# Float16 parts for the first 64 queries of later pairs, bfloat16 products for the scales, and averaged planning deadlines

## The chip, the cores and the metric

The kernel runs on one core of a Trainium2 chip. The metric is the device time of one execution in microseconds. A core has five engines that run side by side: PE (TensorE, matrix products), DVE (VectorE), ACT (ScalarE), POOL (GpSimd) and SP (SyncE, which issues the DMA transfers here). Each engine works through its own instructions in the order in which they were written.

## The reference

Eight batches of eight heads do causal attention over 576 positions of 64 values, with a bias that falls with the running sum of `s`. The result goes through two dense layers with an ELU between them.

```
scores = q @ k.T / 8 + min(-(cum[i] - cum[j]), 0)      # causal, cum = cumsum(max(s, 0))
attn   = softmax(scores)
x      = (attn @ v) with the heads side by side          # 4608 rows of 512
h      = x @ w_in                                        # 512 -> 2048
g      = where(h > 0, h, exp(min(h, 0)) - 1)
out    = g @ w_out                                       # 2048 -> 512, float32
```

## The kernel before

**Arithmetic.** PE takes a float32 product in a slower form than a float16 one. Nearly all products are therefore made from float16 parts: a number is multiplied by a power of two, its rounded float16 value is the high part, what is left over is the low part, and three products (high by high, high by low, low by high) are summed in PSUM. The power of two comes from the largest absolute value of the data.

**Scales.** `scales_of` (L713 on) finds such a power. DVE reduces columns of peaks into one column of `tops` (L723), PE multiplies `tops` by the identity matrix so that the 128 partitions' maxima lie in one row (`flat`, L734), DVE takes the maximum and builds the power of two from its exponent bits (`own`, L726 to L730), PE multiplies a matrix of ones by it so that every partition has it (`every`, L737), and DVE copies it to a column of `scales` (L739). Both products are float32, and the trace shows a float32 product as two matmul records. There are 13 calls: 3 for the early batches, 1 for the weights, 9 for groups of values.

**Attention.** Heads are worked in pairs. For the first three batches (`Low`) the first 320 queries run in float32. For the other five (batches 3 to 7) the first 64 queries of both heads make a unit of their own (`u.h is None`): 20 units. Such a unit scores one 128 by 128 block (`sc_None`, L1141), takes the softmax (`psh_None`, normalised at L1162 to L1166 by whichever engine the planner picks), transposes it on PE (`tr_None`, L1294), splits the transposed block into a rounded part and a rest in the type float32r (`split_pt`, `pc_None`, L1227), and multiplies both by the values (`av_None`, L1287). The values `vs_None` are a rounded part and a rest too (`rounded` at L488 to L490, `rest` at L508 and L509). `halves` (L1350 on) then adds the part that was multiplied by the rounded values to the part multiplied by the rest: a copy (L515) and an addition (L1356) for each head. The later queries run with float16 parts: their probabilities go through DMA transposes (L481) and come back as `T`, which meets the values `v` in `av` (L1328).

**Dense layers.** The 4608 rows are cut into 18 chunks of 256. The first chunk runs in float32 while the weights are still being converted, the others with three float16 products (`h` at L1503, `o` at L1560). The activation between them takes ACT (L1515, L1539) and DVE (L1535, L1542).

**The order of the work.** All of this is first written down as operations (`Plan.op`), each with the engines that could do it and a cost for each. `Plan.run` is a list scheduler: it takes the operation that could start first, and among those of the same engine that could start by then the one with the earliest latest-start time `late`. `Plan.deadlines` works those times out backwards from the end of a finished run. `Plan.issue` does this in rounds:

```
for n in range(self.ROUNDS):                     # 8
    end, order = self.run(False)
    if best is None or end < best[0]:
        best = end, self.wait, [(o, o.late) for o in self.ops]
    self.deadlines(order, end)
```

The times under which the planned end was earliest are used once more to write the instructions out. So every instruction's place in the queue of its engine depends on the costs of all operations. In the first 60 us PE also runs products that nobody reads (`scratch`, L1623), placed where the plan leaves it idle.

Of the kernel before, what the change touches and what calls it, by code (L numbers as in the profile page):

```python
# [93 lines left out]
class Op:  # L94
    __slots__ = ("ways", "after", "before", "behind", "bufs", "new", "prio", "ready", "left", "filler", "late", "at", "frees")


class Plan:
# [45 lines left out]
    def op(self, prio, ways, reads=(), writes=(), late=()):  # L144
# [44 lines left out]
        o.left, o.ready, o.late = len(o.after) + len(firsts), {}, 0.0  # L189
# [21 lines left out]
    def deadlines(self, order, end):  # L211

        late = dict.fromkeys(self.ENDS, end)
        for o in reversed(order):
            engine, start, stop, lag = o.at
            t = late.get(engine, end)
            for d in o.before:
                if d.at is not None:
                    t = min(t, d.late - lag - self.HOPS.get((engine, d.at[0]), self.HOP))
            for b in o.bufs:  # L220
                for d in b.followed:
                    t = min(t, d.late - lag - self.HOPS.get((engine, d.at[0]), self.HOP))
            t -= stop - start
            for d in o.behind:
                if d.at is not None:
                    t = min(t, d.late)
            o.late = t
            if engine in late:
                late[engine] = t

    ENDS = ("PE",)
    ROUNDS, WAIT = 8, {"PE": 0.0, "DVE": 0.0, "ACT": 0.0, "Pool": 0.0, "SP": 0.0}

    def issue(self):
        best = None
        for n in range(self.ROUNDS):
# [7 lines left out]
        for o, late in lates:  # L244
            o.late = late
# [3 lines left out]
    def run(self, emit):  # L249
# [24 lines left out]
        while pending:  # L274
# [13 lines left out]
            for o in pending:  # L288
# [31 lines left out]
                key=lambda x: (x[4].late, x[1]))  # L320
# [76 lines left out]
def act_s(n):  # L397

    return 205 + n / 1.2
# [17 lines left out]
def pool_1(n):  # L417

    return 255 + 0.87 * n
# [8 lines left out]
def kernel(  # L428
# [55 lines left out]
    def rounded(prio, n, dst, src, reads, writes, sign=1.0, only=None):  # L484

        ways = [
            ("Pool", pool_1(n),
             lambda: pool.tensor_scalar(dst(), src(), sign, 1.0, ALU.mult, ALU.mult)),  # L488
            ("ACT", act_s(n),
             lambda: act.activation(dst(), src(), AF.Copy, scale=sign)),  # L490
            ("DVE-SB", dve_1(n),
             lambda: dve.tensor_scalar(dst(), src(), sign, None, ALU.mult)),
        ]
        op(prio, [w for w in ways if only is None or w[0] in only], reads, writes)

# [8 lines left out]

    def rest(prio, n, dst, src, hi, reads, writes, only=None):

        ways = [
            ("DVE-SB", dve_2(n), lambda: dve.tensor_tensor(dst(), src(), hi(), ALU.subtract)),  # L508
            ("Pool", pool_2(n), lambda: pool.tensor_tensor(dst(), src(), hi(), ALU.subtract)),  # L509
        ]  # L510
        op(prio, [w for w in ways if only is None or w[0] in only], reads, writes)
# [163 lines left out]
    all_ones = plan.buf(const, [P, P], F32, "all_ones")  # L675
# [7 lines left out]
    def scale_tiles():  # L683
# [4 lines left out]
        op(-8, [("Pool-M", 150.0, lambda: pool.memset(all_ones.v, 1.0))], [], [all_ones])  # L688

# [23 lines left out]
    def scales_of(prio, spans, dst):  # L713
# [6 lines left out]

        def largest():
# [3 lines left out]
        def exponents():  # L725
# [4 lines left out]
            dve.tensor_scalar(own.v[:, :n], ident[:, :n], own.v[:, 3:4], None, ALU.mult)  # L730
# [366 lines left out]
    def prepare(u):  # L1097
# [17 lines left out]
        src, used = (lambda: u.va.v[:, j, :1]), values_of(u.va, j)  # L1115
        rounded(prio, D, lambda: u.vs.v[:, :1, 0], src, used, [u.vs])
        rest(prio, D, lambda: u.vs.v[:, :1, 1], src,
             lambda: u.vs.v[:, :1, 0].bitcast(F32), used, [u.vs])
# [105 lines left out]
    def split_pt(prio, tag, tr, w):  # L1224
        pc = plan.buf(sb, [P, 2, w], F32R, f"pc_{tag}", tag="pc")
        psum_copy(prio, w, lambda: pc.v[:, 0], lambda: tr.v[:, :w], [tr], [(pc, 0)])
        op(prio, [("DVE", dve_p(w), lambda: dve.tensor_tensor(  # L1227
            pc.v[:, 1], tr.v[:, :w], pc.v[:, 0].bitcast(F32), ALU.subtract))],
# [3 lines left out]
    def scoring(u):  # L1232
# [8 lines left out]
        if u.h is None:  # L1241
# [3 lines left out]
            def pair():  # L1245
# [6 lines left out]
                    (sm, 0, True, 1, 1.0), view=lambda v: v.rearrange("p (h t) -> p h t", h=2),  # L1252
# [26 lines left out]
    def weighing(u):  # L1279
# [11 lines left out]
        if u.h is None:  # L1291
            def pair():
# [4 lines left out]
                products(pe(P), [  # L1297
                    ([pc, u.vs], lambda pc=pc, m=m: (
                        u.vs.v.rearrange("p n a d -> p n (a d)")[:, 0], pc[0].v[:, m]))
                    for m, pc in enumerate(pieces)], slice(P), True, True)  # L1300
                for h in range(2):
                    halves(prio, h, HB, u.x_part((h, 0)), 0, av, h * HB)
# [47 lines left out]
    def halves(prio, h, n, dst, c0, av, a0):  # L1350
# [3 lines left out]
        cols, here = slice(c0, c0 + n), slice(a0, a0 + n)  # L1354
# [375 lines left out]
```

## Time and profile before

| what | value |
|---|---|
| median of 3 runs | 1020.91 us (1017.25 to 1024.87) |
| the profiled execution | 1021.47 us |
| its span, first to last instruction | 1019.7 us |
| PE busy | 997.2 us, 98% of the span |
| DVE busy | 846.5 us, 83% |
| ACT busy | 660.1 us, 65% |
| POOL busy | 261.1 us, 26% |
| mean granted TensorE clock | 0.998 of full speed |

PE is the engine that is nearly always busy. A matmul's record lasts longer than the time until the next matmul can start, because matmuls are pipelined; what a product costs is therefore read from the distance between starts, not from the mean duration. A busy share of 98% leaves about 22 us in which the profile sees PE do nothing, and the stretches in which they lie matter more than their sum.

### The profile page before, as it was taken

The numbers are of one execution on the slowest core, as the hardware profiler recorded it, in microseconds if no ns is written. First come the engines' busy times: TensorE is split into PE (matmuls) and PEld (weight loads), VectorE is DVE, ScalarE is ACT, GpSimd is POOL, SyncE is SP. The second block draws the span as 40 slices with busy tenths as digits, with TensorE's granted clock in tenths as the row PEclk, the third lists the DMA queues.
The fourth block names the chain that finished last, engine by engine and source line by source line (L and its number), as shares of the span: only waits on it lengthen the run. The fifth ranks groups of instructions, "written<-read, shape, count | busy, mean of one in ns | idle before, by whom it ended". The sixth has DMA issues, their size and how long they took to land.

```text
span 1019.7 us, 21777 instructions
## 1 busy us (share of the span) xinstructions
PE 997.2 (98%) x7327; PEld 686.5 (67%) x7327; DVE 846.5 (83%) x2352; ACT 660.1 (65%) x1583; POOL 261.1 (26%) x429
## 2 busy tenths in 40 slices
PE   8999999999989999999999999999999999999998
PEld 7677666666656666666666666666766666666665
DVE  6899899989989898999998998898979898744343
ACT  5999776776667676676776777666657665533232
POOL 6332272423232323322222222221412330100000
PEclk9999999999999999999999999999999999999999
DMA  7888743688999997899889999989979998521000
GB/s 205 251 256 274 208 130 87 133 224 162 195 205 205 225 224 178 191 223 214 184 181 225 199 185 203 239 185 240 189 177 217 204 210 180 92 69 43 1 22 21
DMA packets 296724, 179.83 MB, mean 176 GB/s; under 512 B 209908, under 2 KB 270564, under 8 KB 296612
## 3 DMA queue, kind: packets, MB, share of 16 engines
q1 hardware_dynamic: 296612, 178.45, 76.6%
q8 instruction: 57, 0.93, 0.4%
q14 instruction: 55, 0.45, 0.1%
HBM read 93.08 MB, written 36.81 MB: 127 GB/s over the span
## 4 chain that ended last, share of the span: by engine, by line
PE 45%; DVE 4%; DMA 2%; issue 1%; ACT 1%; SPq 0%; DVEq 0%; ACTq 0%
PE h L1503 19%; PE o L1560 19%; PE sc L1141 3%; PE av L1328 3%; DMA T<-p 1%; DVE p L1209 1%; DVE p L1144 1%; DMA stq<-in_qT_dram 0%; DVE gg L1542 0%; DVE h L1535 0%; DMA spread<-parts 0%; ACT p L1149 0%; DVE p L1203 0%; DVE parts L1064 0%; ACT g L1522 0%
## 5 line engine op out<-in xcount | busy, mean ns | idle before, releaser
L1503 PE MATMUL h<-xh,wp 128*128 128x256 f16 x2176 | 401.5, 273 | 0.0
L1560 PE MATMUL o<-wp,gg 128*128 128x512 f16 x1632 | 391.2, 379 | 4.1 <-DVE tops L723 1.5
L1503 PEld LDWEIGHTS <-wp 128*128 128x128 f16 x3264 | 317.4, 98 | 66.1 <-issue 1.3
L1503 PE MATMUL h<-xl,wp 128*128 128x256 f16 x1088 | 296.9, 273 | 0.0
L1560 PEld LDWEIGHTS <-gg 128*128 128x128 f16 x1632 | 156.8, 98 | 152.8 <-DVE gg L1542 5.9
L1149 ACT ACTIVATE p<-p,mn 128x192 f32<-128x192 f32 (+1 forms) x232 | 144.0, 621 | 80.1 <-DVE mn L1144 77.5
L1209 DVE SCALAR_TENSOR_TENSOR p<-p,sm,p 128x512 f16<-128x512 f32 (+3 forms) x258 | 155.1, 630 | 3.4 <-ACT p L1205 1.5
L1515 ACT ACTIVATE g<-h,cs 128x512 f32<-128x512 f32 x136 | 92.4, 679 | 77.1 <-PE h L1503 75.5
L1539 ACT ACTIVATE gg<-h 128x512 f16<-128x512 f32 x127 | 75.4, 593 | 85.5 <-DVE h L1535 84.7
L1542 DVE SCALAR_TENSOR_TENSOR gg<-h,gg 128x512 f16<-128x512 f32 x136 | 93.2, 685 | 25.0 <-ACT gg L1539 24.5
L1141 PE MATMUL sc<-set 128*128 128x288 f16 (+3 forms) x544 | 109.7, 298 | 2.9 <-DVE mn L1144 1.6
L1144 DVE CUSTOM_DVE_ANT_0 p<-sc,maskw 128x192 f32<-128x192 f32 (+1 forms) x232 | 108.6, 480 | 4.2 <-PE sc L1141 1.8
L1535 DVE SCALAR_TENSOR_TENSOR h<-g,cs,h 128x512 f32<-128x512 f32 x136 | 101.9, 749 | 9.1 <-ACT g L1522 5.2
L1201 POOL TENSOR_SCALAR p<-p,sm 128x512 f16<-128x512 f32 (+3 forms) x78 | 53.6, 691 | 217.6 <-DVE sm L1155 80.3
L1205 ACT ACTIVATE p<-p,sm 128x512 f16<-128x512 f32 (+3 forms) x152 | 79.1, 532 | 26.5 <-ACT p L1149 8.3
L1526 DVE TENSOR_SCALAR g<-g 128x512 f32<-128x512 f32 x81 | 36.3, 448 | 58.1 <-ACT g L1515 57.7
L1141 PEld LDWEIGHTS <-set 128*128 128x128 f16 x584 | 55.1, 98 | 35.8 <-issue 6.0
L1328 PEld LDWEIGHTS <-v 128*64 128x64 f16 x960 | 48.5, 111 | 24.4 <-issue 13.7
L1328 PE MATMUL av<-T,v 128*64 128x256 f16 (+5 forms) x960 | 62.3, 281 | 2.1 <-DMA T<-p 2.0
L500 POOL TENSOR_SCALAR v<-va,scales 128x320 f16<-128x320 f32 (+1 forms) x41 | 25.3, 620 | 98.7 <-PE av L1328 66.8
L500 POOL TENSOR_SCALAR xh<-xc,cs 128x512 f16<-128x512 f32 x22 | 16.7, 760 | 130.0 <-PE h L1503 127.0
L1149 ACT ACTIVATION_READ_ACCUMULATOR p<-p,mn 128x1 f32 x232 | 43.6, 188 | 0.0
(205 smaller groups left out, 1271.2 us busy)
## 6 DMA issues: line engine op xcount, KB each, us to landing
set<-spread SPq DMA_DIRECT2D x32, 432.0 KB
spread<-parts_None SPq DMA_DIRECT2D x32, 288.0 KB
set<-spread SPq DMA_DIRECT2D x32, 288.0 KB
raws<-in_w_in_dram SPq DMA_DIRECT2D x16, 512.0 KB
raws<-in_w_out_dram SPq DMA_DIRECT2D x16, 512.0 KB
out_dram<-ost SPq DMA_DIRECT2D x32, 256.0 KB
va<-in_vb_dram SPq DMA_DIRECT2D x16, 352.0 KB
xc<-x_dram SPq DMA_DIRECT2D x22, 256.0 KB
```

The costliest lines, as they stand in the source:

```text
L1141: pe_.matmul(view(sc.v[:, :cw]), l, r, start=n == 0, stop=n == len(pairs) - 1)
L1144: op(prio, [("DVE", 168 + cw + 55 * (i > 0), lambda i=i, sc=sc: dve.tensor_tensor_reduce(pt.v[:, i * cw : (i + 1) * cw], sc.v[:, :cw], mv( ...
L1149: op(prio, [("ACT", 383 + w / 1.2, lambda: act.activation(pt.v[:, :w], pt.v[:, :w], AF.Exp, bias=mn.v[:, n - 1 : n], scale=-1.0, accum_out ...
L1205: ("ACT", 295 + size / 1.2, lambda part=part: act.activation(part(0), own(part), AF.Copy, scale=sm.v[:, r])),
L1209: ("DVE-SB", dve_2(size), lambda part=part: dve.scalar_tensor_tensor(part(1), own(part), sm.v[:, r], part(0), ALU.mult, ALU.subtract)),
L1328: pe_.matmul(av.v[w.h * HB : (w.h + 1) * HB, dst], w.values.v[:, w.h, kb, v], part(w, kb, m), start=kb == 0 and m == 0 and v == 0, stop=kb ...
L1503: pe_.matmul(columns(k), weight_part(f, 0, part)[1]()[:, c * P : (c + 1) * P], xx.v[:, c], start=(c == 0 and m == 0), stop=(c == NCB - 1 a ...
L1515: op(side, [("ACT", act_c(W) + (0 if native else 90), lambda: act.activation(g.v, hp.v, AF.Exp, scale=1.0 if native else by(3)))], [hp] + ...
L1535: op(side, [("DVE", dve_p(W) + 60, lambda: dve.scalar_tensor_tensor(hp.v, g.v, by(2 if sign[0] else 1), hp.v, ALU.mult, ALU.max))], [g, cs ...
L1539: ("ACT", act_c(W), lambda: act.activation(gg.v[:, 0], hp.v, AF.Copy, scale=2.0**-DOWN)),
L1542: op(side, [("DVE", dve_p(W), lambda: dve.scalar_tensor_tensor(gg.v[:, 1], hp.v, 2.0**-DOWN, gg.v[:, 0], ALU.mult, ALU.subtract))], [hp, ( ...
L1560: pe_.matmul(acc[i].v, gg.v[:, g, at], weight_part(f, 1, part)[1](), start=(f == 0 and m == 0), stop=(f == NF - 1 and m == 2),)
```

## The change

Three things are edited.

1. `scales_of` takes only the upper 16 bits of each maximum (a bfloat16 with the same exponent) and multiplies by a bfloat16 identity `ident16`, a new tile that POOL fills once. The power of two is kept in bfloat16 too, and `all_ones` becomes bfloat16. Each of the two products becomes one matmul of 16-bit data.
2. The 20 first-64 units go to float16. The probabilities carry a factor `UP` of 2^15, the values the group's scale `u.col`, so `vs` now waits for that column of `scales`. Their low part is made by DVE alone (it was DVE or POOL). `pc` is float16 and has its own buffer tag `pt16` in place of the one that it shared with `psh`. `halves` multiplies by the inverse scale in both of its steps.
3. The planner sorts by `due`, which is the mean of the earlier `due` and the new `late` from the second round on, runs 10 rounds in place of 8, and leaves the unread products out of the deadlines.

```
 def deadlines(self, order, end):
...
-                if d.at is not None:
+                if d.at is not None and not d.filler:
...
-    ROUNDS, WAIT = 8, {"PE": 0.0, "DVE": 0.0, "ACT": 0.0, "Pool": 0.0, "SP": 0.0}
+    ROUNDS, WAIT = 10, {"PE": 0.0, "DVE": 0.0, "ACT": 0.0, "Pool": 0.0, "SP": 0.0}
...
-                best = end, self.wait, [(o, o.late) for o in self.ops]
+                best = end, self.wait, [(o, o.due) for o in self.ops]
             self.deadlines(order, end)
+            for o in order:
+                o.due = o.late if not n else (o.due + o.late) / 2
...
-                key=lambda x: (x[4].late, x[1]))
+                key=lambda x: (x[4].due, x[1]))
...
-    all_ones = plan.buf(const, [P, P], F32, "all_ones")
+    all_ones = plan.buf(const, [P, P], BF16, "all_ones")
+    ident16 = plan.buf(const, [P, P], BF16, "ident16")
...
+        def powers():
+            return own.v.bitcast(BF16)[:, :n]
...
-            dve.tensor_scalar(own.v[:, :n], ident[:, :n], own.v[:, 3:4], None, ALU.mult)
+            dve.tensor_scalar(powers(), ident[:, :n], own.v[:, 3:4], None, ALU.mult)
...
-        op(prio, [("PE", pe4(P), lambda: pe_.matmul(flat.v[:, :P], tops.v, ident, start=True, stop=True))],
-           [tops], [flat])
+        op(prio, [("PE", pe16(P) + 60.0, lambda: pe_.matmul(
+            flat.v[:, :P], tops.v.bitcast(BF16)[:, 1::2], ident16.v, start=True, stop=True))],
+           [tops, ident16], [flat])
...
-        op(prio, [("PE", pe4(P), lambda: pe_.matmul(every.v[:, :n], all_ones.v, own.v[:, :n], start=True, stop=True))],
+        op(prio, [("PE", 90.0, lambda: pe_.matmul(every.v[:, :n], all_ones.v, powers(), start=True, stop=True))],
...
-        u.vs = plan.buf(sb, [P, 1, 2, D], F32R, f"vs_{u.tag}", tag="vs0", bufs=NP)
+        u.vs = plan.buf(sb, [P, 2, D], F16, f"vs_{u.tag}", tag="vs0", bufs=NP)
...
+        by = lambda: scales.v[:, u.col : u.col + 1]
+        scaled(prio, D, lambda: u.vs.v[:, 0], src, by, used, [(u.vs, 0)])
+        op(prio, [("DVE-SB", dve_2(D), lambda: dve.scalar_tensor_tensor(
+            u.vs.v[:, 1], src(), by(), u.vs.v[:, 0], ALU.mult, ALU.subtract))], [*used, (u.vs, 0)], [(u.vs, 1)])
...
-        pc = plan.buf(sb, [P, 2, w], F32R, f"pc_{tag}", tag="pc")
+        pc = plan.buf(sb, [P, 2, w], F16, f"pc_{tag}", tag="pt16")
...
-                products(pe(P), [
-                    ([pc, u.vs], lambda pc=pc, m=m: (
-                        u.vs.v.rearrange("p n a d -> p n (a d)")[:, 0], pc[0].v[:, m]))
+                products(pe16(P) + 30.0, [
+                    ([pc, (u.vs, 0), (u.vs, 1)], lambda pc=pc, m=m: (
+                        u.vs.v.rearrange("p a d -> p (a d)"), pc[0].v[:, m]))
...
-        psum_copy(prio, n, lambda: x.v[own, cols], lambda: av.v[other, here], [av], [dst])
-        op(prio, [("DVE", dve_p(n), lambda: dve.tensor_tensor(
-            x.v[own, cols], av.v[own, here], x.v[own, cols], ALU.add))], [av], [dst])
+        op(prio, [
+            ("ACT", act_c(n) + 90, lambda: act.activation(
+                x.v[own, cols], av.v[other, here], AF.Copy, scale=scales.v[other, back])),
+            ("DVE", dve_p(n), lambda: dve.tensor_scalar(
+                x.v[own, cols], av.v[other, here], scales.v[other, back], None, ALU.mult)),
+        ], [av, (scales, back.start)], [dst])
+        op(prio, [("DVE", dve_p(n) + 60, lambda: dve.scalar_tensor_tensor(
+            x.v[own, cols], av.v[own, here], scales.v[own, back], x.v[own, cols], ALU.mult, ALU.add))],
+           [av, (scales, back.start)], [dst])
```

## Rows read from the trace of the kernel before

**Rows 1.** The page, busy us (share of the span) and instructions of PE

```profile
PE 997.2 (98%) x7327; PEld 686.5 (67%) x7327; DVE 846.5 (83%) x2352; ACT 660.1 (65%) x1583; POOL 261.1 (26%) x429
```

**Rows 2.** Stretches: busy PE, PEld, DVE, ACT, POOL (instructions), granted clock, DMA share, GB/s

```profile
0.00:75.00 75.00, 69.52 (x482) 55.14 (x483) 62.69 (x212) 58.82 (x184) 34.37 (x90) 1.00 0.82 237
150.00:200.00 50.00, 47.79 (x361) 33.14 (x361) 48.84 (x141) 34.71 (x93) 19.55 (x28) 1.00 0.49 110
200.00:300.00 100.00, 95.44 (x706) 63.44 (x705) 90.11 (x271) 67.78 (x170) 32.84 (x47) 1.00 0.92 197
300.00:800.00 500.00, 495.79 (x3812) 338.79 (x3810) 451.00 (x1277) 346.75 (x822) 127.22 (x191) 1.00 0.94 204
800.00:900.00 100.00, 97.98 (x773) 68.13 (x772) 80.72 (x208) 58.68 (x121) 18.48 (x29) 0.98 0.80 168
```

**Rows 3.** Waits of PE: us in total, times, longest us

```profile
PE sc L1141 <- DVE mn L1144: 3.0, 5, 0.8
PE tr_None L1294 <- ACT psh_None L1166: 2.2, 1, 2.2
PE av L1328 <- DMA T<-p: 2.0, 1, 2.0
```

**Rows 4.** Lines of PE, the unread products: busy us, mean ns | idle before

```profile
L1623 PE MATMUL scratch<-ident 128*128 128x128 f32 x138 | 20.1, 301 | 0.0
```

**Rows 5.** Products of the first 64 queries: duration ns min/median/max, first and last start

```profile
L1287 PE MATMUL av_None<-pc_None,vs_None x40: 272/292/412, 161.6 to 609.8; 128*128 128x128 f32 x40
```

**Rows 6.** Timeline of PE around 363 us: start us, us, what

```profile
363.22 0.27 PE L1503 MATMUL h<-xl,wp 128*128 128x256 f16 x1
363.33 0.27 PE L1503 MATMUL h<-xh,wp 128*128 128x256 f16 x1
363.36 0.42 PE L1287 MATMUL av_None<-pc_None,vs_None 128*128 128x128 f32 x2
363.61 0.29 PE L1503 MATMUL h<-xh,wp 128*128 128x256 f16 x1
```

**Rows 7.** Timeline of PE and its weight loads at 286.4 us

```profile
286.40 0.28 PE L1141 MATMUL sc_None<-set 128*128 128x128 f16 x2
286.51 0.59 PE L1560 MATMUL o<-wp,gg 128*128 128x512 f16 x2
...
286.40 0.10 PEld L1141 LDWEIGHTS <-set 128*128 128x128 f16 x1
```

**Rows 8.** The scales' products from 150 us on, columns as in Rows 5

```profile
L734 PE MATMUL flat<-ident,tops x16: 272/275/276, 158.3 to 799.5; 128*128 128x128 f32 x16
...
L737 PE MATMUL every<-own,all_ones x16: 167/215/251, 161.0 to 802.2; 128*128 128x1 f32 x16
```

**Rows 9.** Timeline of PE around 649 and 651.5 us

```profile
649.04 0.39 PE L734 MATMUL flat<-ident,tops 128*128 128x128 f32 x2
649.26 0.27 PE L1503 MATMUL h<-xh,wp 128*128 128x256 f16 x1
...
651.54 0.28 PE L737 MATMUL every<-own,all_ones 128*128 128x1 f32 x2
651.68 0.59 PE L1560 MATMUL o<-wp,gg 128*128 128x512 f16 x2
```

**Rows 10.** Lines of POOL, DVE and ACT, columns as in Rows 4

```profile
L509 POOL TENSOR_TENSOR vs_None<-va,vs_None 128x64 fp32r<-128x64 f32 x17 | 7.5, 446 | 5.8 <-ACT vs_None L490 5.1
...
L1535 DVE SCALAR_TENSOR_TENSOR h<-g,cs,h 128x512 f32<-128x512 f32 x136 | 101.9, 749 | 9.1 <-ACT g L1522 5.2
L1542 DVE SCALAR_TENSOR_TENSOR gg<-h,gg 128x512 f16<-128x512 f32 x136 | 93.2, 685 | 25.0 <-ACT gg L1539 24.5
...
L1340 ACT ACTIVATE x_None<-av,scales 128x512 f32<-128x512 f32 x13 | 8.7, 672 | 0.5 <-PE av L1328 0.5
L515 ACT COPY tl<-trl 128x512 f32<-128x512 f32 x8 | 4.6, 578 | 0.6 <-PE trl L938 0.4
```

**Rows 11.** DVE's three rests of the values, columns as in Rows 5

```profile
L508 DVE TENSOR_TENSOR vs_None<-va,vs_None x3: 219/225/226, 93.7 to 389.7; 128x64 fp32r<-128x64 f32 x3
```

More of the change, by code (lines that the diff above doesn't have):

```diff
@@ L94 @@
 class Op:
-    __slots__ = ("ways", "after", "before", "behind", "bufs", "new", "prio", "ready", "left", "filler", "late", "at", "frees")
+    __slots__ = ("ways", "after", "before", "behind", "bufs", "new", "prio", "ready", "left", "filler", "late", "at", "due")
 class Plan:
@@ L188, in op @@
             d.behind.append(o)
-        o.left, o.ready, o.late = len(o.after) + len(firsts), {}, 0.0
+        o.left, o.ready, o.due = len(o.after) + len(firsts), {}, 0.0
         self.ops.append(o)
@@ L224, in deadlines @@
             for d in o.behind:
-                if d.at is not None:
+                if d.at is not None and not d.filler:
                     t = min(t, d.late)
@@ L240, in issue @@
             if best is None or end < best[0]:
-                best = end, self.wait, [(o, o.late) for o in self.ops]
+                best = end, self.wait, [(o, o.due) for o in self.ops]
             self.deadlines(order, end)
+            for o in order:
+                o.due = o.late if not n else (o.due + o.late) / 2
         _, self.wait, lates = best
-        for o, late in lates:
-            o.late = late
+        for o, due in lates:
+            o.due = due
         self.reset()
@@ L482, in turned_load @@
                    units * P * P * 2.2)], reads, writes)
[L484 to L494, printed above, removed]
     def scaled(prio, n, dst, src, by, reads, writes):
@@ L503, in scaled @@
         ], reads, writes)
[L505 to L511, printed above, removed]
     def psum_copy(prio, n, dst, src, reads, writes, only=None):
@@ L688, in scale_tiles @@
         op(-8, [("Pool-M", 150.0, lambda: pool.memset(all_ones.v, 1.0))], [], [all_ones])
+        op(-8, [("Pool", pool_1(P), lambda: pool.tensor_scalar(ident16.v, ident, 1.0, 1.0, ALU.mult, ALU.mult))],
+           [], [ident16])
     junk = const.tile([P, (1 + 2 * (NQ + 1)) * D], BF16, name="junk")
@@ L1111, in prepare @@
         b, j, prio = u.b, u.j, u.prio
-        u.vs = plan.buf(sb, [P, 1, 2, D], F32R, f"vs_{u.tag}", tag="vs0", bufs=NP)
+        u.vs = plan.buf(sb, [P, 2, D], F16, f"vs_{u.tag}", tag="vs0", bufs=NP)
         if u.col == 4:
             prio = PRIO_V
[L1115 to L1118, printed above, removed]
+        src, used = (lambda: u.va.v[:, j, 0]), [*values_of(u.va, j), (scales, u.col)]
+        by = lambda: scales.v[:, u.col : u.col + 1]
+        scaled(prio, D, lambda: u.vs.v[:, 0], src, by, used, [(u.vs, 0)])
+        op(prio, [("DVE-SB", dve_2(D), lambda: dve.scalar_tensor_tensor(
+            u.vs.v[:, 1], src(), by(), u.vs.v[:, 0], ALU.mult, ALU.subtract))], [*used, (u.vs, 0)], [(u.vs, 1)])
     plan.signal = (id(ps), "o0")
@@ L1251, in pair @@
                             "p (h t) -> p h t", h=2)[:, :, :HB]) for q, k in ((Q1, K1), (Q2, K2))],
-                    (sm, 0, True, 1, 1.0), view=lambda v: v.rearrange("p (h t) -> p h t", h=2),
+                    (sm, 0, True, 1, UP), view=lambda v: v.rearrange("p (h t) -> p h t", h=2),
                 )
@@ L1348, in weighing, with halves @@
         return [heads]
-    def halves(prio, h, n, dst, c0, av, a0):
+    def halves(prio, h, n, dst, c0, av, a0, back):
         x = dst[0]
         own, other = slice(h * HB, (h + 1) * HB), slice((1 - h) * HB, (2 - h) * HB)
-        cols, here = slice(c0, c0 + n), slice(a0, a0 + n)
-        psum_copy(prio, n, lambda: x.v[own, cols], lambda: av.v[other, here], [av], [dst])
-        op(prio, [("DVE", dve_p(n), lambda: dve.tensor_tensor(
-            x.v[own, cols], av.v[own, here], x.v[own, cols], ALU.add))], [av], [dst])
+        cols, here, back = slice(c0, c0 + n), slice(a0, a0 + n), slice(back, back + 1)
+        op(prio, [
[7 more added lines that the diff above has]
+           [av, (scales, back.start)], [dst])
     def attention():
```

4 lines of the change are left out of this document (2 added, 2 removed).

## The prediction

> **What bounds the kernel now.** I read the page's busy shares first. PE is at 98%, DVE at 83%, the others far below [rows 1]. So work taken from PE is worth its time wherever PE runs without a gap, and work added elsewhere is worth something only where PE waits for it.
>
> The table of stretches says where that is. In the first 75 us PE has 5.5 us of idle time [rows 2], and 20.1 us more go to products that nobody reads [rows 4]: there PE is not the bound. From 150 us on it is. Its idle time is 2.2 us up to 200, 4.6 up to 300, 4.2 in the next 500 us and 2.0 up to 900, together 13.0 us. In the last of these stretches the granted clock is 0.98, so part of it ran at the lower of the two levels, 1.2 GHz; two hundredths of 100 us are 2 us lost. That makes a reserve of 15 us that a perfect order could give back after 150 us. DVE has 1.2, 9.9 and 49.0 us free in the three stretches from 150 to 800, together 60 us: busy nine tenths, it is second in line.
>
> The waits of PE come next. They are scattered: five waits for the row minimum of the scores make 3.0 us, one wait for a normalisation by ACT in a first-64 unit 2.2, one wait for a DMA transpose 2.0 [rows 3]. No single dependence explains the 13 us; each is a place where the plan came out a little wrong.
>
> **Part 1, products of the first 64 queries.** There are 40, two in each of 20 units, from 161.6 to 609.8 us [rows 5]: all in the stretch that PE bounds. In the timeline one dense-layer matmul starts 0.11 us after the other, but 0.28 us when the pair stands between them, so the pair costs 0.17 us [rows 6]. Two float16 matmuls of the same 128 columns, each with its own weight load, take 0.11 us from the first start to the next instruction's [rows 7]. That saves 0.06 us in each of 20 units, 1.2 us. Bounds: if the two weight loads of 0.10 us were not hidden, the pair would take 0.20 us and the kernel lose 0.6 us; if the whole 0.25 us from the pair's first start to the next instruction's counted, it would gain 2.8 us. I take 1.2, from the row that has the very form.
>
> The Trainium skill (TensorE: Matmul & The Clock Gate, "Back-to-back issue gap") says that in a real stream of weight loads and matmuls the spacing at 128 columns is some 81 ns, because both operations set it. By it the pair would take 0.16 us, this part would save only 0.2 us, and the sum would be 1.0 us longer. The trace speaks against it with 0.055 us for each [rows 7].
>
> **Part 2, the scales.** Of 13 calls 8 lie after 150 us: 16 records of each product, two for each call [rows 8]. A `flat` costs 0.22 us and an `every` 0.14 us from start to the next start [rows 9]. After the change each is one matmul; I price both at the 0.055 us of a 128-column float16 matmul. That saves 8 x 0.165 = 1.3 us and 8 x 0.085 = 0.7 us. No 16-bit matmul of one column is in the trace. Bounds: with a weight load of 0.10 us in the open each would take 0.155, which saves 0.5 and loses 0.1; at no cost at all they would save 1.8 and 1.1. The five earlier calls I cost at nothing: what they free lies where PE has unread products to drop, or ahead of the 2.2 us of waiting between 150 and 200 us. If that cover were gone they would give 1.25 us.
>
> The DVE steps between the two products stay. The new POOL instruction that fills `ident16` runs once, early, on an engine that is free for more than half of the first 75 us.
>
> **Part 3, DVE and ACT.** The low part of `vs` goes from POOL to DVE in 17 of 20 units; on POOL it took 446 ns [rows 10], DVE took 225 ns for the same form [rows 11]. A scale read from memory adds 64 ns, by the 749 ns against the 685 ns of two like instructions with and without it [rows 10]. So DVE gets 17 x 0.29 + 3 x 0.064 = 5.1 us, and 40 x 0.064 = 2.6 us for the additions in `halves`: 7.7 us. The 40 copies in `halves` gain a scale too, 94 ns each on ACT by 672 against 578 ns [rows 10], 3.8 us on an engine that is three tenths idle; I cost this at nothing, and at 3.8 us if the cover fails. The rest of part 2 of the change (types, buffer tags) moves no work. The new buffer for `pc` only frees `psh` from waiting for it.
>
> Queued behind the longer DVE steps are the row minima for which PE waits most often. 7.7 us are 13% of DVE's 60 free microseconds; the waits of PE from 150 to 800 us are 11.0 us, and 13% more of them is 1.4 us. I take this; the ends are nothing and all of 7.7 us.
>
> The new wait of `vs` for its scale stands in the queue of whichever engine makes the high part, and behind it in the transposed units' products. From the first `flat` to the first `every` the chain takes 2.7 us, and 2.7 us for the last [rows 8]. The later queries' values wait for the same column already, so I cost it at nothing. If it came late, it would cost up to 2.7 us for each of five groups.
>
> **Part 4, the order.** New deadlines and new costs move nearly every instruction, on SP's and POOL's queues as well, where the transposes and the loads stand. The trace of before has no row for this. Above, the reserve of 15 us bounds the gain after 150 us. Below, the worst stretch, 200 to 300 us, loses 4.6 us in 100; if all 750 us up to 900 did, that would be 34 us, 21 us more than now. The value I take is 3 us gained, nearer to none than to all: the 500 us up to 800 lose only 4.2 us under the same rules, so an order with few misses exists; but the three large waits are single accidents, and another order has accidents of its own.
>
> **Sum.** Against the profiled execution of 1021.5 us (its span is 1019.7): -1.2 -1.3 -0.7 +1.4 -3.0 = -4.8, so 1016.7 us. That execution lies 0.6 us above the median of the three runs, 1020.9, and well inside their spread. I predict 1016.5.
>
> **Rivals.** First, *the order is what counts*. If it gives back half of the reserve (7.5 us) and DVE's extra work is hidden, the time is 1021.5 - 3.2 - 7.5 = 1010.8; with all of it and the upper bounds of PE's savings, 1001. In favour: the long nearly gapless stretch, and some 25 us of PE time without use in the first 75 us, which I have counted in no term. Against: DVE is nearly full there too, and the deadlines are still worked out from the same costs, so what they misjudge they go on misjudging. Chance 0.20, time about 1008.
>
> Second, *the new deadlines change nothing that matters*: another order, as many accidents. Then only parts 1 to 3 are left, 1019.7 us, and with the lower bounds of PE's savings and all of DVE's increase up to 1029. In favour: the scattered waits. Chance 0.18, most of it between 1018 and 1025.
>
> Third, slower: *DVE becomes the bound between 150 and 800 us*. The row minima then come late throughout as they do from 200 to 300 us. At that stretch's rate the time is 1021.5 - 3.2 + 21 = 1039. It decides from the point where PE's waits after 150 us reach 26 us, twice what they are. Against it: DVE was as busy from 300 to 800 us, and PE waited 4.2 us there. Chance 0.06.
>
> **Numbers.** The forecast itself (1011 to 1020) has the remaining 0.56. The range is 1007 to 1025: it takes in the forecast, the second rival and half of the first, and leaves out some 0.16. One per cent, about what a measurement of this kernel can tell from no change, is 1010.7 below and 1031.1 above. So faster is the first rival's 0.20, slower the third's 0.06, and within 1% the 0.74 between them.
>
> **What would show it.** Part 1: the pair of `av_None` matmuls in 0.11 us between two dense-layer matmuls, not 0.16 or more. Part 2: half as many records of `flat` and `every`, each some 0.06 us. Part 3: 20 DVE instructions for the low part of `vs`, none on POOL, and no longer list of PE's waits for row minima. Part 4: PE's idle time after 150 us near 10 us, with other waits at its head than now. The prediction is wrong if that idle time is under 6 or over 20 us, or if the first 75 us end with clearly fewer unread products and the rest begins earlier.

## The result and the profile after

The changed kernel takes 1030.05 us (median of 6 runs, 1028.33 to 1032.93), the kernel before, measured beside it, 1019.67 us (6 runs, 1017.25 to 1024.87). The ratio is 1.0101, with an interval from 1.0072 to 1.0131: the change costs about 1%. The prediction was 1016.5 us with a range that ended at 1025.0. Its direction was wrong and the time lies outside its range.

The profiled execution of the changed kernel took 1029.07 us, with a span of 1027.3 us: 7.6 us more than the span before. Its busy times, columns as in [rows 1]:

```profile
PE 998.9 (97%) x7301; PEld 677.1 (66%) x7301; DVE 845.2 (82%) x2358; ACT 677.0 (66%) x1605; POOL 255.2 (25%) x410
```

DVE is no busier than before, although the change gives it work. The new plan moved other work off it: ACT has 16.9 us more. So the longer span isn't more work on the engine that was second in line.

The stretches of the changed kernel, columns as in [rows 2]:

```profile
0.00:75.00 75.00, 68.94 (x471) 53.31 (x472) 62.08 (x209) 58.26 (x181) 33.85 (x88) 1.00 0.81 237
150.00:200.00 50.00, 46.89 (x348) 31.05 (x346) 48.76 (x135) 34.35 (x85) 12.03 (x18) 1.00 0.47 115
200.00:300.00 100.00, 97.67 (x727) 64.98 (x726) 89.56 (x276) 69.48 (x168) 30.10 (x44) 1.00 0.92 197
300.00:800.00 500.00, 487.32 (x3741) 329.40 (x3739) 448.25 (x1265) 355.23 (x834) 131.11 (x192) 1.00 0.96 203
800.00:900.00 100.00, 99.75 (x787) 67.97 (x786) 83.82 (x227) 63.27 (x131) 18.92 (x26) 1.00 0.81 176
```

PE's idle time from 150 to 900 us is 3.1 + 2.3 + 12.7 + 0.3 = 18.4 us; it was 13.0. It fell where it had been worst (200 to 300 us, 4.6 to 2.3) and tripled in the long stretch that had run almost without a gap (4.2 to 12.7). The granted clock is 1.00 in the last stretch, where it was 0.98. PE's waits, columns as in [rows 3]:

```profile
PE sc L1132 <- DVE mn L1135: 9.7, 19, 1.7
PE o L1557 <- DVE gg L1539: 2.4, 5, 0.7
...
PE every L727 <- DVE own L719: 1.8, 2, 1.2
...
PE flat L723 <- DVE tops L712: 1.2, 3, 0.6
...
PE av L1319 <- DMA T<-p: 0.5, 1, 0.5
```

The wait for the row minimum of the scores has gone from 3.0 us in 5 waits to 9.7 us in 19. Two accidents of before are gone (the 2.2 us for a normalisation, and 1.5 of the 2.0 us for a transpose), and PE now waits for DVE in other places, among them the products of the scales (`every` and `flat`).

The changed operations, first those of part 1 and 2, then those of part 3 (columns as in [rows 5]):

```profile
L1278 PE MATMUL av_None<-pc_None,vs_None x40: 216/219/219, 164.2 to 618.8; 128*128 128x128 f16 x40
...
L723 PE MATMUL flat<-ident,tops x8: 219/219/232, 159.3 to 803.4; 128*128 128x128 bf16 x8
...
L727 PE MATMUL every<-own,all_ones x8: 163/167/167, 162.2 to 806.3; 128*128 128x1 bf16 x8
...
L1108 DVE SCALAR_TENSOR_TENSOR vs_None<-va,scales,vs_None x20: 254/278/1299, 111.2 to 520.7; 128x64 f16<-128x64 f32 x20
...
L1352 DVE SCALAR_TENSOR_TENSOR x_None<-av_None,scales,x_None x40: 263/284/292, 171.9 to 625.3; 64x64 f32<-64x64 f32 x40
...
L1347 ACT ACTIVATE x_None<-av_None,scales x35: 307/311/312, 165.8 to 623.9; 64x64 f32<-64x64 f32 x35
```

And PE's timeline around one pair and one call of the scales, columns as in [rows 6]:

```profile
470.49 0.28 PE L1278 MATMUL av_None<-pc_None,vs_None 128*128 128x128 f16 x2
470.60 0.38 PE L1557 MATMUL o<-wp,gg 128*128 128x512 f16 x1
...
662.32 0.22 PE L723 MATMUL flat<-ident,tops 128*128 128x128 bf16 x1
662.38 0.29 PE L1132 MATMUL sc<-set 128*128 128x288 f16 x1
...
664.58 0.17 PE L727 MATMUL every<-own,all_ones 128*128 128x1 bf16 x1
664.60 0.27 PE L1500 MATMUL h<-xh,wp 128*128 128x256 f16 x1
```

The pair takes 0.11 us (0.17 before), a `flat` 0.06 (0.22), an `every` 0.03 (0.14; the two starts above are rounded, the median of all eight is 0.028). So each product became as cheap as was said or cheaper.

**An account of the 7.6 us**, from the starts of PE's matmuls in both traces. A gap is here what the distance between two starts has beyond 0.42 ns for each column, the spacing of the 128-column and 512-column float16 products in both traces (0.055 and 0.215 us). The first `o` of the first float16 chunk, at about 149 us, starts 2.8 us later. After 150 us there are 42 gaps of over 0.25 us, 24.8 us together, against 17 with 15.3: +9.5. The cheaper products give -3.4 (20 x 0.06 + 8 x 0.164 + 8 x 0.112). A stretch at half clock that followed the 2.0 us wait for the transpose (810 to 813.4 us, granted clock 0.50, the level of 1.2 GHz) is gone: -1.7. That last term belongs to these two executions: the profiles of the same changed kernel in experiments 8 and 15 have such a stretch of 3.4 us too. Together +7.2. The loss isn't one event: it is many more small gaps, and 2.8 us that are lost before the first `o`.

**Where one of the larger gaps comes from.** PE and then DVE, in the changed kernel's timelines around 605 us (a time in brackets is what the instruction waited, and for whom):

```profile
605.22 0.81 PE L1557 MATMUL o<-wp,gg 128*128 128x512 f16 x3
607.75 0.40 PE L1132 MATMUL sc<-set 128*128 128x288 f16 x2 [1.72 <-DVE mn L1135]
```

```profile
603.98 0.57 DVE L1352 SCALAR_TENSOR_TENSOR x_None<-av_None,scales,x_None 64x64 f32<-64x64 f32 x2
606.61 0.42 DVE L684 TENSOR_REDUCE pk<-stq 128x1 f32<-128x256 f32 x1 [2.06 <-DMA stq<-in_qT_dram]
607.06 0.62 DVE L1135 CUSTOM_DVE_ANT_0 p<-sc,maskw 128x448 f32<-128x448 f32 x1
```

The planner gave DVE the largest absolute value (`pk`) of a block of queries (`stq`). The load had not landed; DVE stood in front of it for 2.06 us with the row minimum (L1135) queued behind, whose scores had been ready since 604.5 us, and PE waited for that. At 739.7 us the same happens again (DVE waits 2.40 us, PE 1.01). Which engine makes these sixteen maxima is the plan's choice. In the kernel before ACT made 14 of them and DVE two; here are ACT's (columns as in [rows 4]):

```profile
L702 ACT ACTIVATE junk<-stq 128x256 bf16<-128x256 f32 x14 | 5.7, 408 | 5.2 <-DMA stq<-in_qT_dram 5.2
```

In the changed kernel DVE makes seven of them and ACT these nine:

```profile
L687 ACT ACTIVATE junk<-stq 128x256 bf16<-128x256 f32 x9 | 3.7, 408 | 2.4 <-DMA stq<-in_qT_dram 2.4
```

ACT waits for late loads as well (5.2 us before), but no row minimum is in its queue.

### The profile page after: what moved, and what is told of

It reads as the page before. It is cut to its first block, busy times and chain, and to the rows that moved or that the text cites. A ratio compares the mean times of both kernels' runs of the same rounds, so it can differ in the third digit from the quotient of the medians.

```text
span 1027.3 us, 21790 instructions
## 1 busy us (share of the span) xinstructions
PE 998.9 (97%) x7301; PEld 677.1 (66%) x7301; DVE 845.2 (82%) x2358; ACT 677.0 (66%) x1605; POOL 255.2 (25%) x410
## 5 line engine op out<-in xcount | busy, mean ns | idle before, releaser
L1200 DVE SCALAR_TENSOR_TENSOR p<-p,sm,p 128x512 f16<-128x512 f32 (+3 forms) x254 | 150.5, 619 | 6.1 <-ACT p L1196 3.2
L1536 ACT ACTIVATE gg<-h 128x512 f16<-128x512 f32 x131 | 77.9, 595 | 93.7 <-DVE h L1532 92.7
L1132 PE MATMUL sc<-set 128*128 128x288 f16 (+3 forms) x544 | 112.0, 297 | 9.1 <-DVE mn L1135 8.6
L1135 DVE CUSTOM_DVE_ANT_0 p<-sc,maskw 128x192 f32<-128x192 f32 (+1 forms) x232 | 109.0, 479 | 10.0 <-PE sc L1132 4.9
L1192 POOL TENSOR_SCALAR p<-p,sm 128x512 f16<-128x512 f32 (+3 forms) x68 | 45.7, 675 | 196.2 <-DVE sm L1146 93.3
L1196 ACT ACTIVATE p<-p,sm 128x64 f16<-128x64 f32 (+3 forms) x153 | 80.6, 538 | 18.4 <-ACT p L1140 8.0
L1523 DVE TENSOR_SCALAR g<-g 128x512 f32<-128x512 f32 x73 | 33.0, 452 | 57.7 <-ACT g L1512 57.6
L490 POOL TENSOR_SCALAR v<-va,scales 128x320 f16<-128x320 f32 (+1 forms) x43 | 29.0, 676 | 104.3 <-PE av L1319 101.6
L1519 ACT ACTIVATE g<-g 128x512 f32<-128x512 f32 x71 | 44.5, 626 | 1.5
```

The costliest lines, as they stand in the source:

```text
L1132: pe_.matmul(view(sc.v[:, :cw]), l, r, start=n == 0, stop=n == len(pairs) - 1)
L1135: op(prio, [("DVE", 168 + cw + 55 * (i > 0), lambda i=i, sc=sc: dve.tensor_tensor_reduce(pt.v[:, i * cw : (i + 1) * cw], sc.v[:, :cw], mv( ...
L1196: ("ACT", 295 + size / 1.2, lambda part=part: act.activation(part(0), own(part), AF.Copy, scale=sm.v[:, r])),
L1200: ("DVE-SB", dve_2(size), lambda part=part: dve.scalar_tensor_tensor(part(1), own(part), sm.v[:, r], part(0), ALU.mult, ALU.subtract)),
L1536: ("ACT", act_c(W), lambda: act.activation(gg.v[:, 0], hp.v, AF.Copy, scale=2.0**-DOWN)),
```

## Experiments

The theories: (O) the new order costs the time, whatever the arithmetic; (P) the new parts cost it, by DVE's longer steps; (R) the averaged deadlines are to blame, and a kernel with the old rule would be as fast as before; (M) loads that land late in front of DVE are the cause. The expectations call P theory D (its two halves D1 and D2) and R theory A; theory L in them says that the order of before is a lucky one. To take order and arithmetic apart, the order of one kernel's plan was recorded (operation, engine, buffer) and replayed in the other. The edit that does it, in `Plan.run`:

```
-            first = min(found, key=lambda x: x[:2])
...
+            for o in sorted(pending, key=lambda o: place[o][0]):   # place: the recorded list
+                # take the first one whose recorded buffers are free
...
+            n = min(place[o][1], len(o.ways) - 1)                  # on the recorded engine
```

Where units with float16 parts run in the old order, twelve operations on `vs` stand a little later than recorded, since their scale isn't known yet at the recorded place. Old parts in the new order keep the buffer tag `pt16` for `pc`. Ratios are to the kernel before on the same chip, with 95% intervals.

**1. New parts, old order.** The changed kernel with the replay, `ORDER` recorded from the kernel before.

> The changed arithmetic (float16 units, bfloat16 scales) with every instruction in the place and on the engine that the plan of the kernel before gave it; 12 operations that build values of a group before its scale is known stand a little later. Theory O (the loss comes with the new order): PE's shorter products are kept and nothing else, 1015 to 1021 us. Theory D (the loss comes with the arithmetic, through the steps that went to DVE and ACT): 1027 to 1033 us. Between the two: the fixed order of before does not suit the new durations.

Measured: 1.0010 (0.9993 to 1.0027). PE's first wait and the whole stretch from 150 to 900 us:

```profile
PE sc L1306 <- DVE mn L1309: 4.6, 9, 1.1
```

```profile
150.00:900.00 750.00, 735.43 (x5626) 497.33 (x5627) 674.08 (x1906) 511.25 (x1200) 192.49 (x279) 1.00 0.89 192
```

With the old order the loss is gone. But the gain isn't there either: the ratio that parts 1 to 3 of the sum give, 0.998, lies below the interval. PE has 14.6 us of idle time instead of 13.0; that is 1.6 us more, about half of the 3.4 us that its products save.

**2. Old parts, new order.** The kernel before with the replay, `ORDER` recorded from the changed kernel, and

```
-        pc = plan.buf(sb, [P, 2, w], F32R, f"pc_{tag}", tag="pc")
+        pc = plan.buf(sb, [P, 2, w], F32R, f"pc_{tag}", tag="pt16")
```

> The arithmetic of before (float32r units, float32 scales) in the order and on the engines of the plan of the changed kernel; the low part of the values is on DVE as there. Theory O: as slow as the changed kernel or up to 4 us slower, 1029 to 1035 us. Theory D: the additions without a scale and the copies without one give their time back, 1018 to 1023 us.

Measured: 1.0038 (1.0017 to 1.0058). Waits of PE:

```profile
PE sc L1317 <- DVE mn L1320: 7.5, 10, 1.6
...
PE flat L910 <- DVE tops L899: 1.4, 3, 0.8
...
PE every L913 <- DVE own L906: 1.2, 2, 0.9
```

Waits of DVE:

```profile
DVE pk L875 <- DMA stq<-in_qT_dram: 5.0, 2, 2.9
```

The order alone costs 0.4% without any of the new arithmetic, and brings the same waits with it: for row minima, for DVE's steps of the scales, and DVE's for loads. That speaks for O and against P as the only cause.

**3. New parts, old rule.** The changed kernel, planned by the rule of before:

```
-                if d.at is not None and not d.filler:
+                if d.at is not None:
...
-    ROUNDS, WAIT = 10, ...
+    ROUNDS, WAIT = 8, ...
...
-                o.due = o.late if not n else (o.due + o.late) / 2
+                o.due = o.late
```

> The changed arithmetic planned by the rule of before: deadlines of the last round alone, 8 rounds. Its order is a third one. Theory A (averaging the deadlines is what makes the order bad): 1015 to 1021 us. Theory O in its plain form (any new order is a new draw, whatever the rule): anywhere from 1016 to 1034 us. Theory D: 1026 to 1033 us.

Measured: 1.0060 (1.0037 to 1.0082). Waits of PE:

```profile
PE sc L1132 <- DVE mn L1135: 6.4, 11, 1.0
```

**4. Old parts, new rule.** The kernel before with the reverse edit.

> The arithmetic of before planned by the new rule: averaged deadlines, 10 rounds, unread products left out of the deadlines. Theory A: 1026 to 1034 us. Theory O in its plain form: anywhere from 1017 to 1034 us. Theory D: 1018 to 1022 us, as before.

Measured: 1.0062 (1.0042 to 1.0083), row minima 6.8 us in 11 waits. R falls: the new arithmetic under the old rule and the old arithmetic under the new rule are both 0.6% slower than the kernel before. In experiment 3 DVE has no wait for `stq` at all, so M can't be the whole cause either. Where its profile loses says more: the first `o` comes at 154.3 us in place of 149.4, and from there to the end it takes 870.7 us against 870.3 before. So nearly all of its loss lies ahead of the first `o`, and of the stretch behind it, where the loads of `stq` are, this run doesn't rule M out.

**5. The kernel before, in the order of its third round.** No arithmetic and no rule is changed; the planner only keeps another of its own eight orders, whose planned end is 1.0 us later by the planner's own clock.

```
-            if best is None or end < best[0]:
+            if n == 2:
```

> The kernel before with nothing changed but which of its own eight rounds of planning is written out: the third, whose planned end is 1.0 us later than that of the fourth, which the kernel uses. Theory L (the order of before is a lucky one, and any other order of equal planned quality is slower on the chip): 1.003 to 1.010 of before. Theory O in its plain form, with no luck in before: as often faster as slower, 0.995 to 1.005. If the plan's own figure were to be trusted: 1.001.

Measured: 1.0036 (1.0018 to 1.0054). Waits of PE, then of DVE:

```profile
PE sc L1141 <- DVE mn L1144: 6.7, 11, 1.8
```

```profile
DVE pk_None L699 <- DMA stq_None<-in_qT_dram: 5.1, 1, 5.1
```

Another order of the same kernel loses 0.4%, with late row minima at the head of PE's list again. The order of before is better than this one of its own kind, though the planner sees 1.0 us between them.

**6. and 7. One part at a time in the old order.** Both are the replay of experiment 1, with the float32 lines of one part put back: 6 keeps only `scales_of` changed, 7 only the first-64 units.

```
# 6                                           # 7
-  u.vs = plan.buf(... F16, ...)              -  ident16, powers(), tops ... bitcast(BF16)
+  u.vs = plan.buf(... F32R, ...)             +  ident, own, tops (float32)
```

> Only the bfloat16 products of the scales, in the order of before. If the shorter products keep their whole value in a fixed order: 2.0 to 2.8 us less, a ratio of 0.997 to 0.998. If in that order other waits take their place: 0.999 to 1.001.

> Only the float16 parts of the first-64 units, in the order of before (12 operations stand later, as in the run with both). Prediction by the terms of the sum: 1.2 us less from PE, up to 1.4 us more from DVE, a ratio of 0.999 to 1.001. If the steps that went to DVE cost more in the fixed order: 1.002 to 1.005. Together with the scales alone this should make up the 1.001 of the run with both.

Measured: 6 has 0.9989 (0.9967 to 1.0011), with 2.8 us of row-minimum waits and 10.1 us of idle time; 7 has 1.0051 (1.0036 to 1.0066), with 5.6 and 17.0 us. The scales alone may save the 0.1 to 0.2% that part 2 promised, but that can't be told from nothing. The units alone seemed to cost 0.5%, which would revive P.

**8. and 15. The changed kernel again,** unedited, in two later comparisons.

> The changed kernel as it is, on the same chip as the others, as the reference for them: 1.007 to 1.013 of before. Old parts in this order gave 1.004: if the arithmetic itself costs time in this order, this is above that by more than the intervals; if not, it lies within 1.002 to 1.006.

> The changed kernel as it is, beside the run with the low part on POOL: 1.0075 to 1.010.

Measured: 1.0075 (1.0054 to 1.0095), and 1.0097 (1.0075 to 1.0120). The loss is real, and 0.75 to 1.0% is as well as its size is known.

**9. Units only, old order, low part on POOL as before.** P's first suspect is taken away:

```
-   ("DVE-SB", dve_2(D), lambda: dve.scalar_tensor_tensor(u.vs.v[:, 1], src(), by(), u.vs.v[:, 0], ...))
+   ("DVE-SB", ...as above...),
+   ("Pool", pool_1(D) + pool_2(D), on_pool)     # scale into vt, subtract the high part
```

> The float16 units alone in the order of before, as in the run that gave 1.005, but the low part of the values is made by POOL in the 17 units where the kernel before had it there (two POOL instructions through a small tile of their own). Theory D1 (DVE's 17 extra instructions of some 0.28 us are what costs): 0.999 to 1.002. If they are not: 1.004 to 1.006.

Measured: 1.0001 (0.9978 to 1.0024), row minima 3.7 us.

**10. The kernel before with more DVE work,** in its own recorded order; behind each of the 40 additions in `halves` stands an instruction whose result nobody reads. It was expected to take 0.15 us; the trace has 0.22 us each, 8.9 us in all (columns as in [rows 4]).

```
+   dve.tensor_tensor(x.v[own, cols], av.v[own, here], x.v[own, cols], ALU.add)
+   dve.tensor_scalar(extra, ident[:, :n], 2.0, None, ALU.mult)
```

```profile
L1536 DVE TENSOR_SCALAR extra<-ident 128x64 f32<-128x64 f32 x40 | 8.9, 222 | 0.6
```

> The kernel before in its own order, with one more small DVE instruction (64 columns, into a tile that nobody reads) behind each of the 40 additions in halves: 40 x some 0.15 us, 6 us of DVE work and nothing else. Theory D (PE pays for DVE work nearly in full): 1.004 to 1.006. The prediction's rate of 0.18 us for each us of DVE: 1.001. If DVE's idle time takes it all: 0.999 to 1.001.

Measured: 1.0018 (0.9998 to 1.0037), that is 1.8 us (-0.2 to +3.8) for 8.9 us of DVE instructions. At this rate the prediction's 7.7 us would cost 1.6 us (it said 1.4); the interval includes that, and nothing as well.

**11. Units only, old order, `halves` without a scale** (it rounds the values and probabilities of the first 64 queries to float16 without scaling them first, and the copies of `halves` lose their scale too):

```
-   by = lambda: scales.v[:, u.col : u.col + 1]
+   by = lambda: scales.v[:, 2:3]                # a column of ones
...
-   x.v[own, cols], av.v[own, here], scales.v[own, back], x.v[own, cols], ALU.mult, ALU.add
+   x.v[own, cols], av.v[own, here], x.v[own, cols], ALU.add
```

> The float16 units alone in the order of before, with the copies and additions of halves as they were, without a scale; so that the values keep their size, the parts are made with a scale of one, and lose low bits. Theory D2 (the 0.06 us on DVE and 0.10 us on ACT that the scale adds in 40 places each cost the time): 0.999 to 1.002. If they don't: 1.004 to 1.006.

Measured: 1.0003 (0.9983 to 1.0023). So the 0.5% of experiment 7 is in neither 9 nor 11, and P looked alive.

**12. Scales only, with a plan of its own.** Experiment 6 without the replay, the rule of before. By the planner's own clock this plan ends 1.9 us *earlier* than that of the kernel before.

> Only the bfloat16 products of the scales, planned anew by the rule of before; its planned end is 1.9 us earlier than that of the kernel before. Theory L (the order of before is a lucky one): 1.002 to 1.008. If orders of equal planned quality are equal on the chip: 0.996 to 0.999, and the best version so far.

Measured: 1.0031 (1.0011 to 1.0052); in experiment 6 the same arithmetic had 0.9989. Waits of PE, then of DVE:

```profile
PE sc L1149 <- DVE mn L1152: 10.2, 13, 2.1
```

```profile
DVE pk L702 <- DMA stq<-in_qT_dram: 5.0, 4, 2.6
```

This part of the change takes work from PE and adds none to DVE, and still loses when its own plan orders it. An earlier planned end didn't mean an earlier end.

**13. and 14. Low part on POOL, with both parts,** in the old order and in the new one (the edit of 9 in experiment 1, and in the changed kernel with its own order replayed).

> Both parts of the changed arithmetic in the order of before, with the low part of the values on POOL as before. If order and DVE's extra instructions are the whole loss, PE's savings are left: 0.997 to 0.999, the best version. If PE's savings are worth nothing in a fixed order: 0.999 to 1.001.

> The changed kernel in its own order, with the low part of the values on POOL in the 17 units where the kernel before had it there. If DVE's extra instructions make up what the arithmetic costs in this order: 1.003 to 1.005, like the old parts in this order (1.004). If that cost lies elsewhere: 1.007 to 1.010, like the changed kernel beside it.

Measured: 13 has 1.0010 (0.9986 to 1.0033), the same as experiment 1 with that work on DVE. 14 has 1.0078 (1.0057 to 1.0099), and 15, the changed kernel beside it, 1.0097 (1.0075 to 1.0120): the intervals overlap. So moving the low part away brings back nothing that could be told from zero where the whole change is in. Experiment 7's 0.5% stands alone against 1, 9, 11 and 13; I don't build on it.

**16. The changed kernel with slower loads in its plan.** If the plan believes in slower loads, it puts their readers later, and DVE shouldn't stand in front of them:

```
-LAG, RATE = 4000.0, 285.0
+LAG, RATE = 4000.0, 240.0
```

> The changed kernel planned with 240 bytes per ns for the DMA engines in place of 285, all else as it is, so that operations on loaded data stand later in the queues of DVE and ACT; the planned end is 23 us later. Theory M (the order loses time where DVE stands at an instruction whose load has not landed, with row minima queued behind it): faster than the changed kernel, 1.000 to 1.005 of before. If late loads are not what the order loses by: 1.006 to 1.025.

Measured: 1.0130 (1.0109 to 1.0152). DVE's wait for `stq` is gone as intended. But the first `o` starts 12.7 us later than before, at 162.2 us. Waits of PE:

```profile
PE sc L1132 <- DVE mn L1135: 11.9, 10, 4.6
```

As a remedy this edit fails: without those waits the kernel got slower. Yet all of the loss lies ahead of the first `o`. From there to the end the profile takes 870.0 us, against 870.3 in the kernel before and 875.1 in the changed one. So the run doesn't speak against M for that stretch; as the whole plan changed, it doesn't show either what the waits alone are worth.

**17. and 18. One part at a time in the new order,** the edits of 6 and 7 with the changed kernel's order.

> The order of the changed kernel, with the bfloat16 products of the scales and the float32r units of before. Old parts throughout gave 1.004 in this order, new parts throughout 1.0075 to 1.010. If the units are what costs in this order: 1.001 to 1.004. If it is the scales: 1.007 to 1.010. If the order costs this much whatever the arithmetic: 1.006 to 1.010 here and in the run with the units alone.

> The order of the changed kernel, with the float16 units and the float32 products of the scales. If the units are what costs: 1.007 to 1.012. If they are not: 1.003 to 1.005, as with old parts throughout. If the order costs this much whatever the arithmetic: 1.006 to 1.010.

Measured: 1.0063 (1.0042 to 1.0084) and 1.0064 (1.0042 to 1.0087), row minima 8.2 us in both. Waits of DVE in 17:

```profile
DVE pk L878 <- DMA stq<-in_qT_dram: 6.7, 2, 4.5
```

The scales alone had 0.9989 in the old order and have 1.0063 in the new one. Nothing differs but the order (and the buffer tag of `pc`).

**What the runs show together.** All kernels in the order of before (1, 6, 7, 9, 10, 11, 13) lie between 0.999 and 1.005, six of the seven at 1.002 or less; their row-minimum waits are 2.8 to 5.6 us. All others, in the new order (2, 8, 14, 15, 17, 18) or in five further ones (3, 4, 5, 12, 16), lie between 1.003 and 1.013, with row-minimum waits of 6.4 to 11.9 us. The two groups don't overlap in these waits. The best version found is experiment 6, scales only in the old order, and it can't be told from the kernel before.

## Why the prediction was wrong

**Part 1 and the PE side of part 2: the sizes were right, their worth was not.** 0.11 us for the pair was predicted and measured, 0.055 us for a `flat` against 0.056, and `every` came out at 0.028, half of what was said. Together 3.4 us of PE time after 150 us, where 3.2 were forecast. The Trainium skill's 81 ns at 128 columns (TensorE: Matmul & The Clock Gate, "Back-to-back issue gap") doesn't hold here either: 0.055 us was measured for each. What failed is that the saving was taken as time. With both parts in an order that stays as it is (experiments 1 and 13) the ratio is 1.001, where parts 1 to 3 together promised 0.998. Experiment 1's profile shows 1.6 us more of idle time and 1.6 us more of waiting for row minima (4.6 against 3.0), as if PE came earlier to a product that waits for DVE. That is not shown for the scales by themselves: in experiment 6 the idle time is 10.1 us, less than before, and its interval (0.9967 to 1.0011) includes the full 2.0 us of part 2 as well as nothing.

**Part 3: the durations were right, and the new order hid their sum.** The low part takes DVE 278 ns (0.29 was said), the scale in `halves` adds 62 ns on DVE (284 against 222; 64 said) and 103 ns on ACT (311 against 208; 94 said). The rows of before for the last two (columns as in [rows 5]):

```profile
L1356 DVE TENSOR_TENSOR x_None<-av_None,x_None x40: 196/222/229, 166.0 to 617.4; 64x64 f32<-64x64 f32 x40
L515 ACT COPY x_None<-av_None x37: 203/208/211, 162.4 to 616.0; 64x64 f32<-64x64 f32 x37
```

All twenty low parts went to DVE and none to POOL. DVE's busy time didn't rise by 7.7 us, though; from 150 to 900 us it is 670.4 us against 670.7, since the new plan gave other work to ACT. In the old order it did rise, from 846.5 us over the whole span to 850.7 (experiment 1) and 853.6 (experiment 7). What such work costs stays open: 1.8 us for 8.9 us of added instructions, with an interval that includes zero (experiment 10). The wait of `vs` for its scale, costed at nothing, is in neither PE's nor DVE's list of waits; POOL and ACT do wait for that column before they make `vs` (7.3 and 0.8 us), on engines that aren't full.

**Part 4, the step that failed.** The prediction put the new order at 3 us gained, between a gain of 15 us and a loss of 21, both counted after 150 us alone, because "an order with few misses exists" and the large waits are accidents. Measured with the old arithmetic, the order costs 0.38% (0.17 to 0.58), about 4 us; with one part in it 0.6%, with both 0.75 to 1.0%. So the term had the wrong sign, and it is larger than all others. How the loss grows from 0.4% to 1% as the parts go in, when the parts cost 0.1% in the old order, isn't settled: some of it may be that they were compared on different chips.

The error in the reasoning: the order of before was treated as one draw among equals. Its trace said otherwise: 4.2 us of idle time in 500 us is what a good order looks like. The text read that row as proof that a good order exists, where it was proof that the kernel *had* it, and another order was more likely to lose some of it than to add to it. The five further plans lost 0.3 to 1.3%, among them one of the same kernel (5) and one with less PE work and no more on DVE (12).

**What a worse order looks like was half foreseen.** The second rival said: another order, as many accidents, 1019.7 up to 1029. The third said that row minima come late throughout and decide from 26 us of idle time on. What came lies between them: late row minima, 19 waits in place of 5, and 18.4 us of idle time. So the mechanism of the third rival appeared without its cause, since DVE isn't busier. Three things come with the new order in every profile of it, and none needs the new arithmetic, since experiment 2 has them all:

- DVE stands in front of a load that has not landed, 4.4 to 6.7 us (at most 1.0 in the old order). At two places of the changed kernel's profile this costs PE 1.72 and 1.01 us.
- PE waits 2.6 to 3.7 us for DVE's steps of the scales, `tops` and `own` (1.5 to 1.9 in the old order).
- The first `o` comes at 152.0 to 155.5 us (149.1 to 152.3 in the old order). This part lies ahead of 150 us, for which the prediction had no term of the order.

How much of the loss each makes was not measured: no run takes one away and leaves the rest in place. For late loads there is a hint. Of the plans other than the old order, the two without any wait of DVE for `stq` (3 and 16) take 870.7 and 870.0 us from the first `o` to the end, as the kernel before does (870.3), experiment 4 with 3.1 us of it takes 871.4, and the nine profiles with 4.4 to 6.7 us take 872.8 to 878.7. These are single executions, and two profiles of the old order (7 and 11) take 874.9 and 878.1 us with at most 1.0 us of such waits. **Why the order of before has so few late row minima stays open.**

**The list of what would show it** did its work. The pair, the records and the twenty DVE instructions came as written; "no longer list of waits for row minima" and "other waits at its head" failed at once and pointed to DVE's place in the order. The unread products stayed at 138. The idle time of 18.4 us lies inside the band of 6 to 20 that was called harmless. That band was too wide: it let a loss of 5 us pass.

## What to carry to other kernels

When the bounding engine is 98% busy and a planner writes the order, an edit of costs or deadlines is a new draw against an order that the trace already shows to be good: price it as a loss, with the spread of the other orders that the same planner makes (0.3 to 1.3% in the five tried here), and not as an even chance. The part ahead of the full stretch needs a term of its own. Take order and arithmetic apart before judging either, by replaying the recorded order; here that showed in two runs what no list of waits could. Time saved on the bounding engine inside a fixed order isn't time saved until it is measured there: here 3.4 us of PE time, with some 7 us of work added to DVE, came to nothing that could be told from zero.

## What the runs showed of the hardware that was not expected

A bfloat16 product of one column, with its own weight load, held PE for 0.028 us until the next start, half the time of one with 128 columns (0.056). And one and the same kernel, the one before, ran between 1017.3 and 1029.6 us over all comparisons at a mean granted clock of 0.993 to 1.0: a single execution can't tell 1% from nothing, and the profiled execution of experiment 6 (span 1014.9 us) looked like a gain of 5 us that its median didn't bear out.
